# A fused recurrence and two gated MLPs on one core: zero products in TensorE's early gaps, a one-byte waste output, a new order table

## The chip, the cores and the metric

One core of a Trainium2 chip. The metric is the device time of one launch in microseconds (us). Three runs of the kernel before took 920.43 to 921.10 us, median 921.01.

## What is computed

A gated linear recurrence per head (4 batches, 8 heads, 768 steps, head size 48), then two MLPs over 3072 tokens of width 384 with 2048 hidden units:

```
for t in range(S):
    state = alpha[:, :, t, :, None] * state + einsum('bhd,bhe->bhde', k[:, :, t], v[:, :, t])
    y[:, :, t] = einsum('bhd,bhde->bhe', q[:, :, t], state)
x = y as (3072, 384)
h = x @ w_in;  x = (h * tanh(softplus(h))) @ w_out      # first MLP
h = x @ w_in2; x = (h * cos(h)) @ w_out2                # second MLP
```

The weights come as 64-bit floats, the rest in fp32.

## The kernel before, in words

**Recurrence.** 12 chunks of 64 steps, each in two halves of the batch; (u, hb) is chunk u, half hb. For each of the 24 pieces the load queue (SP) brings alpha (`ld_a`), keys (`ld_k`), queries (`ld_q`) and values (`ld_v`, `ld_vt`). VectorE (DVE) forms the running products of alpha (`scan`, L405), their backward form (`scan2`, L423), scales keys (`keys`, L427) and queries (`queries`, L437). TensorE (PE) forms `scores` (L469), DVE masks them (`causal`, L477 to L480), PE makes `out_mm` (L490 to L494), transposes the keys (`turn`, L455) and makes the new state (`state_mm`, L552, L559), which `state_mul` (L579 to L583) scales. `guard` (L413, ScalarE or ACT) looks whether every alpha is large enough for this path: the sum of relu(0.79 - alpha) goes to `alow`, the elementwise result to a waste tile `junk` that nobody reads.

**MLPs.** Blocks of 512 tokens; each 128-wide slice of the hidden layer is one step. `mm1` (L631 to L633) makes h from x and the weights in nine one-pass products (x and the weights are each split in a high and a low fp32r part). ACT and DVE make the gate (`angle`, `sines`, `gated`), `act_c` (L670, L672) and `pool_c` (L677) split the result in two, and `mm2` (L692 to L694) adds nine products into three accumulators `acc0` to `acc2`. The first six slices of the first block are taken in pairs over 256 tokens: mm1(0) to mm1(2) need the recurrence's (0,0) and (0,1), mm1(3) to mm1(5) need (1,0) and (1,1).

**Bridge.** For chunks 0 to 3, `last_heads` (L499) and `fill` (L505) bring the last two heads to their place, `y_hi` (L513) and `y_lo` (L519) write the two parts of x, for which mm1 waits.

**Weights.** `ld_w` loads slice fc of a layer (768 KB), and six passes `conv_x`, `conv_s` (L322), `conv_b`, `conv_c` (L335), `conv_d` (L340 on DVE) and `conv_e` (L348) turn the 64-bit numbers into the high and low parts. Tables (`TOPS`, `SCALES`, `ROUNDS`, `LOWS`) choose the engine of each.

**What sets the order.** All pieces are listed with an engine, and the table `ORDER` (2398 numbers) gives the sequence in which they are written out; every engine and the load queue run their own pieces strictly in that sequence. `VCOPY`, `QPOOL`, `KPOOL`, `MULS`, `GLS`, `CASTS` choose engines for other pieces. `IDLE` is 0, so no `idle` piece (L617) is written out. Buffers tie the loads to the engines: there is one buffer for keys and one for alpha, so `ld_k` of a piece waits for `scores` and `turn` of the piece before, and `ld_a` for its `keys`.

Of the kernel before, what the change touches and what calls it, by code (L numbers as in the profile page):

```python
# [13 lines left out]
F32 = mybir.dt.float32  # L14
F32R = mybir.dt.float32r
# [96 lines left out]
)  # L112
VCOPY = {*range(0, 4), *range(6, 24)}
LOAD_K = 143.22
LOAD_Q = -93.756
LOAD_V = -90.03
# [123 lines left out]
def chunked_path(ctx: ExitStack, tc: tile.TileContext, q, k, alpha, v1, ve, vo, w1, w2, const, out):  # L240
# [5 lines left out]
    def stile(shape, dtype, tag, name):  # L246
        return sb.tile(shape, dtype, tag=tag, bufs=BUFS[tag], name=name)
# [906 lines left out]
```

## Time and profile before

| | |
|---|---|
| runs, median (range) | 921.01 us (920.43 to 921.10) |
| the profiled execution | 920.94 us, of which span 919.0 us from first to last instruction |
| TensorE (PE) busy | 892.6 us, 97% of the span |
| DVE, ACT, POOL busy | 584.7, 655.8, 310.6 us |
| mean granted clock of TensorE | 0.987 of full speed |

A granted clock of 1.00 is 2.4 GHz, 0.50 is 1.2 GHz. The page's row of 40 slices of 23 us shows the clock under 1.00 in the first two slices alone (0.8 and 0.6), and PE's first slice at 4 tenths busy, its second at 8; from the third on it is at 9, but for the last (7). So what is not yet filled lies in the first 50 us.

### The profile page before, as it was taken

The page shows a single profiled execution, that of the slowest core. Times are in us where ns is not written, and L with a number is a line of the kernel's source. Part 1 is how long each engine was busy: PE and PEld are TensorE (multiplying, and loading weights), DVE is VectorE, ACT ScalarE, POOL GpSimd, SP SyncE. Part 2 cuts the span into 40 slices and gives each one's busy share as a digit, 9 for nine tenths or more (in the row PEclk, how much of TensorE's full clock was granted, in tenths as well). Part 3 has the DMA queues.
Part 4 walks back from the last instruction along what each step waited for, and adds up shares of the span by engine and source line. Part 5 has one row for each costly group of instructions (what it writes and reads, how often), then busy time and mean ns, then how long its engine had stood idle before and what let it go on. Part 6 is the DMA issues. An engine that isn't in the chain of part 4 may idle for free.

```text
span 919.0 us, 15379 instructions
## 1 busy us (share of the span) xinstructions
PE 892.6 (97%) x6038; PEld 734.2 (80%) x6038; DVE 584.7 (64%) x863; ACT 655.8 (71%) x1032; POOL 310.6 (34%) x237
## 2 busy tenths in 40 slices
PE   4899999999999999999999999999999999999997
PEld 3788787878878888788888888888888888888886
DVE  7999987575556467543687986865545445444552
ACT  3799798887869978988999856566545646555552
POOL 3655454121225033433266563333212124011021
PEclk8699999999999999999999999999999999999999
DMA  8866411212112213220133221200000000000001
GB/s 238 261 191 210 136 30 44 72 56 63 59 51 83 69 55 97 74 78 1 39 102 100 70 70 35 69 0 36 12 24 0 35 1 1 35 0 1 35 1 36
DMA packets 25325, 59.08 MB, mean 64 GB/s; under 512 B 3872, under 2 KB 7840, under 8 KB 25248
## 3 DMA queue, kind: packets, MB, share of 16 engines
q1 hardware_dynamic: 25104, 57.92, 20.2%
q8 instruction: 48, 0.79, 0.4%
q14 instruction: 29, 0.24, 0.1%
q10 hardware_dynamic: 144, 0.13, 0.0%
HBM read 52.53 MB, written 4.72 MB: 62 GB/s over the span
## 4 chain that ended last, share of the span: by engine, by line
PE 91%; DVE 4%; DMA 2%; ACT 1%; issue 1%; SPq 1%; DVEq 0%; ACTq 0%
PE h L631 14%; PE acc L692 14%; PE acc L694 14%; PE acc L693 14%; PE h L633 14%; PE h L632 14%; PE y L493 2%; PE sc L469 2%; DMA qt<-in_q_chunks_dram 1%; PE dS L559 1%; PE pt L455 1%; DVE wr L322 1%; DMA vt<-in_v_chunks_dram 1%; DVE wr L335 1%; DVE Pt L405 0%
## 5 line engine op out<-in xcount | busy, mean ns | idle before, releaser
L677 POOL TENSOR_TENSOR gl<-ta,gh 128x512 fp32r<-128x512 f32 x97 | 142.0, 1466 | 374.0 <-DVE gh L670 201.7
L631 PE MATMUL h<-xhi,wh 128*128 128x512 f32 (+1 forms) x594 | 233.2, 393 | 0.0
L692 PE MATMUL acc<-gh,wh 128*128 128x512 f32 (+1 forms) x594 | 229.9, 387 | 0.0
L633 PE MATMUL h<-xhi,wl 128*128 128x512 f32 (+1 forms) x594 | 229.0, 385 | 0.0
L632 PE MATMUL h<-xlo,wh 128*128 128x512 f32 (+1 forms) x594 | 228.9, 385 | 0.0
L694 PE MATMUL acc<-gl,wh 128*128 128x512 f32 (+1 forms) x594 | 227.5, 383 | 0.0
L693 PE MATMUL acc<-gh,wl 128*128 128x512 f32 (+1 forms) x594 | 227.4, 383 | 0.0
L631 PEld LDWEIGHTS h<-xhi,wh 128*128 128x128 f32 x594 | 113.0, 190 | 23.6 <-DVE ta L647 0.7
L633 PEld LDWEIGHTS h<-xhi,wl 128*128 128x128 f32 x594 | 113.0, 190 | 22.3
L632 PEld LDWEIGHTS h<-xlo,wh 128*128 128x128 f32 x594 | 113.1, 190 | 20.6
L692 PEld LDWEIGHTS acc<-gh,wh 128*128 128x128 f32 x594 | 111.6, 188 | 22.4 <-issue 0.6
L694 PEld LDWEIGHTS acc<-gl,wh 128*128 128x128 f32 x594 | 111.6, 188 | 22.2
L693 PEld LDWEIGHTS acc<-gh,wl 128*128 128x128 f32 x594 | 111.6, 188 | 21.2
L659 DVE SCALAR_TENSOR_TENSOR tb<-tb,ta 128x512 f32<-128x512 f32 x96 | 79.9, 833 | 74.4 <-ACT tb L656 74.3
L652 ACT ACTIVATE ta<-h 128x512 f32<-128x512 f32 x96 | 57.3, 597 | 84.5 <-PE h L633 48.4
L647 DVE TENSOR_TENSOR ta<-h,ta 128x512 f32<-128x512 f32 x96 | 64.9, 685 | 58.8 <-ACT ta L644 58.3
L677 DVE TENSOR_TENSOR gl<-ta,gh 128x512 fp32r<-128x512 f32 x95 | 75.4, 794 | 34.0 <-ACT gh L672 31.1
L662 ACT ACTIVATE tb<-tb 128x512 f32<-128x512 f32 x96 | 60.4, 629 | 48.3 <-DVE tb L659 48.3
L665 DVE TENSOR_TENSOR ta<-h,tb 128x512 f32<-128x512 f32 x96 | 66.0, 687 | 30.3 <-ACT tb L662 29.9
L670 DVE CAST gh<-ta 128x512 fp32r<-128x512 f32 x106 | 54.7, 519 | 43.4 <-PE acc L693 42.6
L672 ACT CAST gh<-ta 128x512 fp32r<-128x512 f32 x86 | 52.7, 616 | 32.3 <-PE acc L693 27.9
L639 ACT ACTIVATE ta<-h 128x512 f32<-128x512 f32 x96 | 57.4, 597 | 25.2 <-PE h L633 15.5
(152 smaller groups left out, 1202.1 us busy)
## 6 DMA issues: line engine op xcount, KB each, us to landing
wr<-in_w_dram SPq DMA_DIRECT2D x16, 768.0 KB, 5.8
three<-in_w_dram SPq DMA_DIRECT2D x16, 768.0 KB, 4.2
at<-in_alpha_chunks_dram SPq DMA_DIRECT2D x23, 227.9 KB, 2.8
qt<-in_q_chunks_dram SPq DMA_DIRECT2D x23, 224.0 KB, 3.4
kt<-in_k_chunks_dram SPq DMA_DIRECT2D x23, 224.0 KB, 2.7
vt<-in_v_chunks_dram SPq DMA_DIRECT2D x21, 192.0 KB, 2.8
out_dram<-o SPq DMA_DIRECT2D x14, 256.0 KB, 2.0
three<-in_ve_chunks_dram SPq DMA_DIRECT2D x24, 128.0 KB, 3.5
```

The lines of the kernel that those rows point to most:

```text
L631: nc.tensor.matmul(h, hi[:, f], xh, start=kc == 0, stop=False)
L632: nc.tensor.matmul(h, hi[:, f], xl, start=False, stop=False)
L633: nc.tensor.matmul(h, lo[:, f], xh, start=False, stop=kc == 2)
L639: nc.scalar.activation(ta_[i], h_[i], AF.Sigmoid, scale=-1.0)
L647: nc.vector.tensor_tensor(ta_[i], h_.pop(i), ta_[i], op=ALU.mult)
L659: nc.vector.scalar_tensor_tensor(out=tb_[i], in0=tb_[i], scalar=MAGIC, in1=ta_[i], op0=ALU.subtract, op1=ALU.subtract)
L662: nc.scalar.activation(tb_[i], tb_[i], AF.Sin, scale=-TWO_PI)
L665: nc.vector.tensor_tensor(ta_[i], h_.pop(i), tb_.pop(i), op=ALU.mult)
L677: eng.tensor_tensor(gl_[i], ta_.pop(i), gh_[i].bitcast(F32)[:, :], op=ALU.subtract)
L692: nc.tensor.matmul(acc[d][:, c0:c1], hi[:, f], gh, start=first, stop=False, skip_group_check=True)
L693: nc.tensor.matmul(acc[d][:, c0:c1], lo[:, f], gh, start=False, stop=False, skip_group_check=True)
L694: nc.tensor.matmul(acc[d][:, c0:c1], hi[:, f], gl, start=False, stop=last, skip_group_check=True)
```

## The change

- `idle` gets operands of its own: a tile of 128x128 zeros, written once by POOL, is both the weights and (four times repeated) the 512 moving columns of a one-pass product into the bank of `acc0`. `IDLE` goes from 0 to 60; an `idle` that comes in the order behind the first mm2 writes nothing, so 22 products are written out.
- `guard` multiplies by a million before the relu, and its waste output is one byte wide instead of two.
- `ORDER` and all tables that choose engines are new. The last 724 numbers of the order are those of before. Two estimates inside the planner change (`turn`, `fill`), which do nothing when the order is read from the table.

```diff
-    (the 2398 numbers of ORDER)
+    (2420 numbers, 22 of them idle pieces)
...
-VCOPY = {*range(0, 4), *range(6, 24)}
+VCOPY = {*range(0, 24)}
...
-LOWS = {*((0, fc) for fc in (2, 4, 7, 10, 13, 14,)), *((1, fc) for fc in (1, 4, 5, 7, 8, 11, 12, 13,))}
+LOWS = {*((0, fc) for fc in (0, 3, 5, 7, 9, 10, 11, 13, 14, 15,)), *((1, fc) for fc in (0, 1, 2, 4, 6, 7, 8, 11, 12, 13,))}
...
-IDLE = 0
+IDLE = 60
...
-TOPS = "aaaappaaappavvpp", "aapapppvavaapava"
-SCALES = "vvaaaaaaapavppvv", "vpvvvpapvppppvpa"
-ROUNDS = "vppaaavvpapapppa", "vvvpvpvpaapavpvv"
+TOPS = "avpvvaaaapavpppv", "vvpvpvapvvpvpava"
+SCALES = "vaaapapapvvaavaa", "vvaavpvpvppvpvpa"
+ROUNDS = "aavaaappaavppvvp", "pppvapvppaaavpvv"
...
+    zeros = sb.tile([P, P], F32R, name="zeros")
+    nc.gpsimd.memset(zeros.bitcast(F32), 0.0)
...
-    nc.vector.memset(abias, AOK)
+    nc.vector.memset(abias, 1e6 * AOK)
...
-        junk = stile([112, NSEG, C], BF16, "junk", "junk")
+        junk = stile([112, NSEG, C], mybir.dt.uint8, "junk", "junk")
...
-        nc.scalar.activation(junk, seg3(at_[s])[:, :, 1:65], AF.Relu, scale=-1.0, bias=abias[:112], accum_out=alow[:, n : n + 1])
+        nc.scalar.activation(junk, seg3(at_[s])[:, :, 1:65], AF.Relu, scale=-1e6, bias=abias[:112], accum_out=alow[:, n : n + 1])
...
-            nc.tensor.matmul(w[0:112], seg_start[:, 0:112], seg_start[:, 0:N], start=True, stop=True, skip_group_check=True)
+            nc.tensor.matmul(w.rearrange("p (a b) -> p a b", b=P), zeros, zeros.unsqueeze(1).to_broadcast([P, 4, P]), start=True, stop=True, skip_group_check=True)
```

**First place: the load queue's first rows.** Names as in the program: `at` is alpha, `big` holds all of piece (0,1), `wr` the raw weights. Before, then changed:

```order
L367 DMA at<-in_alpha_chunks_dram 112x521
L367 DMA big<-in_alpha_chunks_dram 112x521
L377 DMA qt<-in_q_chunks_dram 112x512
L959 DMA cst<-in_const_dram 128x272
L372 DMA kt<-in_k_chunks_dram 112x512
L380 DMA three_73<-in_ve_chunks_dram 64x512
L381 DMA three_73<-in_vo_chunks_dram 64x512
L372 DMA big<-in_k_chunks_dram 112x512
L303 DMA wr<-in_w_dram 128x1536
L367 DMA at<-in_alpha_chunks_dram 112x521
L377 DMA big<-in_q_chunks_dram 112x512
L303 DMA wr<-in_w_dram 128x1536
```
```order
L370 DMA at<-in_alpha_chunks_dram 112x521
L370 DMA big<-in_alpha_chunks_dram 112x521
L306 DMA wr<-in_w_dram 128x1536
L380 DMA qt<-in_q_chunks_dram 112x512
L375 DMA kt<-in_k_chunks_dram 112x512
L375 DMA big<-in_k_chunks_dram 112x512
L962 DMA cst<-in_const_dram 128x272
L383 DMA three_75<-in_ve_chunks_dram 64x512
L384 DMA three_75<-in_vo_chunks_dram 64x512
L380 DMA big<-in_q_chunks_dram 112x512
L394 DMA vt<-in_v_chunks_dram 128x384
L370 DMA at<-in_alpha_chunks_dram 112x521
```

The first weights moved from ninth to third place, ahead of the first queries and keys; the values `vt` that the first state products read moved ahead of the second alpha and the second weights.

**Second place: PE, from the first out_mm to the first state products** (`y` is out_mm's bank, `dS` the state's, `zeros` the fill operand). Before, then changed:

```order
L491 MATMUL y<-three_74,three_73 64x64
L455 MATMUL pt<-cst,big 128x112 x4
L559 MATMUL dS_192<-vt,kT 48x48 x2
L559 MATMUL dS_193<-vt,kT 48x48 x2
L505 MATMUL y<-st_180,cst 32x128 x6
```
```order
L494 MATMUL y<-three_76,three_75 64x64
L623 MATMUL acc_200<-zeros 128x512
L623 MATMUL acc_203<-zeros 128x512
L623 MATMUL acc_206<-zeros 128x512
L623 MATMUL acc_209<-zeros 128x512
L623 MATMUL acc_212<-zeros 128x512
L623 MATMUL acc_216<-zeros 128x512
L562 MATMUL dS_219<-vt,kT 48x48 x2
```

Six fill products now stand between the two; five more stand ahead of everything, four ahead of fill(0,0), two ahead of out_mm(0,1), four ahead of mm1(0), and one ahead of state_mm(0,1).

**Third place: DVE's last rows up to keys(2,0), and PE's around the first mm2.** (`ta<-h,ta` is gated(0), `gl` is pool_c(0), `wl` a conv_e, the last `kt` keys(2,0).) DVE before, then changed:

```order
L579 TENSOR_TENSOR three_73<-dS_460,aend 48x4x48 x2
L579 TENSOR_TENSOR three_73<-dS_461,aend 48x4x48 x2
L405 SCALAR_TENSOR_TENSOR Pt<-at,seg_start 112x520
L322 SCALAR_TENSOR_TENSOR wr<-wr 128x768
L647 TENSOR_TENSOR ta<-h,ta 128x512
L409 RECIPROCAL rend<-Pt 112x8
L335 SCALAR_TENSOR_TENSOR wr<-wr 128x768
L423 SCALAR_TENSOR_TENSOR at<-at,rend 112x520
L427 TENSOR_TENSOR kt<-kt,at 112x512
L348 TENSOR_TENSOR wl<-wr,wh 128x768
L677 TENSOR_TENSOR gl<-ta,gh 128x512
```
```order
L351 TENSOR_TENSOR wl<-wr,wh 128x768
L650 TENSOR_TENSOR ta<-h,ta 128x512
L338 SCALAR_TENSOR_TENSOR wr<-wr 128x768
L412 RECIPROCAL rend<-Pt 112x8
L680 TENSOR_TENSOR gl<-ta,gh 128x512
L338 SCALAR_TENSOR_TENSOR wr<-wr 128x768
L426 SCALAR_TENSOR_TENSOR at<-at,rend 112x520
L430 TENSOR_TENSOR kt<-kt,at 112x512
L351 TENSOR_TENSOR wl<-wr,wh 128x768
```

PE before (the end of scores(2,0), fill(1,1), mm2(0)), then changed (the end of mm1(1), fill(1,1), scores(2,0)):

```order
L470 MATMUL sc<-three_73,kt 64x64
L505 MATMUL y<-st_585,cst 32x128 x6
L692 MATMUL acc_603<-gh,wh 128x256
L693 MATMUL acc_603<-gh,wl 128x256
L694 MATMUL acc_603<-gl,wh 128x256
```
```order
L634 MATMUL h<-xhi,wh 128x256
L635 MATMUL h<-xlo,wh 128x256
L636 MATMUL h<-xhi,wl 128x256
L508 MATMUL y<-st_599,cst 32x128 x6
L472 MATMUL sc<-three_75,kt 64x64
```

pool_c(0) moved ahead of keys(2,0) on DVE, and on PE fill(1,1) ahead of scores(2,0), so that mm2(0) follows scores(2,0) at once.

## Rows read from the trace of the kernel before

**Rows 1.** Windows: engines' busy us (instructions), granted clock, DMA share, GB/s
```profile
17.90:35.20 17.30, 15.09 (x202) 13.16 (x203) 15.59 (x21) 10.91 (x21) 9.81 (x7) 0.51 0.94 271
35.20:50.00 14.80, 11.02 (x184) 9.51 (x184) 14.55 (x21) 12.15 (x22) 7.87 (x5) 0.77 0.72 229
50.00:70.00 20.00, 19.30 (x294) 17.20 (x290) 18.98 (x31) 18.87 (x29) 11.97 (x7) 1.00 0.59 183
70.00:100.00 30.00, 29.58 (x404) 25.15 (x403) 27.84 (x39) 24.32 (x42) 16.03 (x13) 1.00 0.59 193
100.00:110.00 10.00, 9.55 (x80) 7.11 (x77) 9.78 (x12) 9.38 (x14) 5.91 (x5) 1.00 0.27 81
```
**Rows 2.** Waits of PE, 110 to 900 us: who for whom, total, times, longest
```profile
PE y L493 <- ACT st L530: 1.1, 1, 1.1
```
**Rows 3.** DVE in order of time: start, us, line, operation [idle before <- releaser]
```profile
19.00 0.95 DVE L335 SCALAR_TENSOR_TENSOR wr<-wr 128x768 uint32<-128x768 uint32 x1
...
21.98 0.56 DVE L340 CAST wh<-wr 128x768 fp32r<-128x768 f32 x1
...
23.79 2.15 DVE L335 SCALAR_TENSOR_TENSOR wr<-wr 128x768 uint32<-128x768 uint32 x1
...
34.59 1.37 DVE L427 TENSOR_TENSOR kt<-kt,at 112x512 f32<-112x512 f32 x1 [0.93 <-DMA kt<-in_k_chunks_dram]
...
48.95 0.69 DVE L427 TENSOR_TENSOR kt<-kt,at 112x512 f32<-112x512 f32 x1
...
50.43 0.69 DVE L677 TENSOR_TENSOR gl<-ta,gh 128x512 fp32r<-128x512 f32 x1
```
**Rows 4.** PE in order of time, 14 to 52 us
```profile
18.46 0.89 PE L559 MATMUL dS<-vt,kT 64*48 64x48 f32 x32 [3.54 <-DMA vt<-in_v_chunks_dram]
...
32.34 0.58 PE L631 MATMUL h<-xhi,wh 128*128 128x256 f32 x1
...
33.15 0.41 PE L631 MATMUL h<-xhi,wh 128*128 128x256 f32 x1
33.36 0.41 PE L632 MATMUL h<-xlo,wh 128*128 128x256 f32 x1
...
35.04 0.28 PE L631 MATMUL h<-xhi,wh 128*128 128x256 f32 x1
...
49.79 0.24 PE L469 MATMUL sc<-three,kt 48*64 48x64 f32 x1 [0.50 <-DVE kt L427]
...
50.87 0.84 PE L505 MATMUL y<-st,cst 48*32 48x128 f32 x12
51.65 0.39 PE L692 MATMUL acc<-gh,wh 128*128 128x256 f32 x1
```
**Rows 5.** Loads issued from 26 to 29 us: KB, us from issue to landing
```profile
kt<-in_k_chunks_dram SPq DMA_DIRECT2D x1, 224.0 KB, 8.4
```
**Rows 6.** Windows of 5 us, columns as in rows 1
```profile
15.00:20.00 5.00, 1.54 (x40) 1.38 (x42) 4.84 (x7) 1.00 (x5) 3.66 (x2) 0.79 1.07 255
20.00:25.00 5.00, 4.44 (x63) 3.67 (x60) 4.32 (x6) 3.84 (x10) 2.37 (x1) 0.50 0.74 209
25.00:30.00 5.00, 3.91 (x60) 3.40 (x60) 4.96 (x6) 3.30 (x5) 4.01 (x4) 0.50 0.99 284
```
**Rows 7.** PE in order of time, steady stage, into an out_mm
```profile
172.36 0.39 PE L632 MATMUL h<-xlo,wh 128*128 128x512 f32 x1
172.59 0.39 PE L633 MATMUL h<-xhi,wl 128*128 128x512 f32 x1
172.91 0.27 PE L493 MATMUL y<-three 128*64 128x64 f32 x1
```
**Rows 8.** Window, columns as in rows 1: attention products alone
```profile
22.00:24.00 2.00, 2.00 (x34) 1.73 (x34) 2.00 (x5) 1.00 (x3) 1.37 (x1) 0.50 0.82 184
```
**Rows 9.** POOL and ACT in order of time: a conv_e, and a guard
```profile
22.63 2.50 POOL L348 TENSOR_TENSOR wl<-wr,wh 128x768 fp32r<-128x768 f32 x1 [3.96 <-DVE wh L340]
...
3.75 0.72 ACT L415 ACTIVATE junk<-at,abias 112x512 bf16<-112x512 f32 x1 [1.73 <-DMA at<-in_alpha_chunks_dram]
```

More of the change, by code (lines that the diff above doesn't have):

```diff
@@ L126 @@
 FILL = 4
-QPOOL = {1, *range(4, 6), *range(7, 9), 12, 15, *range(19, 23)}
-MULS = {3, 5, *range(7, 9), *range(10, 13), 14, 18, *range(20, 22)}
-LOWS = {*((0, fc) for fc in (2, 4, 7, 10, 13, 14,)), *((1, fc) for fc in (1, 4, 5, 7, 8, 11, 12, 13,))}
-GLS = {0, *range(2, 9), *range(12, 14), *range(17, 22), *range(23, 25), 26, *range(28, 31), 33, *range(35, 37), 39, 41, *range(45, 47), *range(48, 50), 51, 53, *range(55, 58), 63, *range(68, 70), 72, 74, *range(76, 78), *range(83, 85), 88, *range(91, 94), *range(98, 100), 101, 106, *range(111, 113), *range(114, 116), 117, *range(121, 124), *range(126, 128), 130, *range(134, 139), 140, *range(142, 144), 146, *range(150, 152), 153, 157, *range(159, 163), *range(164, 166), 169, *range(173, 178), *range(179, 181), *range(185, 188), 189, *range(191, 193), *range(194, 199)}
-IDLE = 0
-KPOOL = {1, 6, *range(8, 11), *range(13, 16), 17, 19, 23}
-TOPS = "aaaappaaappavvpp", "aapapppvavaapava"
-SCALES = "vvaaaaaaapavppvv", "vpvvvpapvppppvpa"
-ROUNDS = "vppaaavvpapapppa", "vvvpvpvpaapavpvv"
+QPOOL = {*range(3, 6), *range(7, 13), 14, 18, 21, 23}
+MULS = {3, 5, *range(7, 9), 10, 12, *range(14, 16), *range(19, 22)}
+LOWS = {*((0, fc) for fc in (0, 3, 5, 7, 9, 10, 11, 13, 14, 15,)), *((1, fc) for fc in (0, 1, 2, 4, 6, 7, 8, 11, 12, 13,))}
+GLS = {0, *range(2, 4), 7, *range(10, 14), 15, 18, 20, *range(22, 24), *range(26, 28), *range(29, 31), 33, 35, *range(37, 40), 41, 43, 46, 48, 52, *range(54, 61), 62, *range(64, 66), *range(67, 69), *range(70, 72), 73, *range(75, 78), *range(79, 83), 84, *range(92, 94), *range(96, 99), *range(100, 105), 106, *range(111, 113), *range(114, 116), 117, *range(121, 124), *range(126, 128), 130, *range(134, 139), 140, *range(142, 144), 146, *range(150, 152), 153, 157, *range(159, 163), *range(164, 166), 169, *range(173, 178), *range(179, 181), *range(185, 188), 189, *range(191, 193), *range(194, 199)}
+IDLE = 60
+KPOOL = {1, 6, 9, *range(11, 14), 15, 18, 22}
+TOPS = "avpvvaaaapavpppv", "vvpvpvapvvpvpava"
+SCALES = "vaaapapapvvaavaa", "vvaavpvpvppvpvpa"
+ROUNDS = "aavaaappaavppvvp", "pppvapvppaaavpvv"
 TICK, BUSY = 10.24 / 3, 3060
@@ L138 @@
 QUARTER = float(np.nextafter(np.float32(np.pi / 2), np.float32(0.0)))
-CASTS = {*range(0, 3), *range(4, 8), 11, 13, *range(16, 18), 19, 26, *range(28, 30), *range(34, 36), *range(37, 39), *range(42, 45), *range(46, 50), *range(51, 53), 54, 56, 58, *range(63, 65), *range(67, 70), 72, *range(79, 82), 86, 89, 95, *range(98, 101), *range(102, 104), 106, 109, 116, *range(118, 121), *range(122, 124), *range(125, 127), *range(129, 131), *range(134, 138), 141, *range(143, 145), 147, *range(151, 154), *range(156, 160), 163, 165, 167, *range(169, 171), *range(173, 175), 178, 181, 185, 189, 192, *range(194, 200)}
+CASTS = {0, 2, *range(5, 8), 9, *range(11, 13), *range(19, 21), 22, *range(24, 27), 28, 30, 36, 38, 41, 48, 52, *range(55, 57), 58, *range(64, 68), 69, 74, 78, 81, 85, 87, 90, 95, 97, 99, *range(102, 104), *range(105, 107), 109, 116, *range(118, 121), *range(122, 124), *range(125, 127), *range(129, 131), *range(134, 138), 141, *range(143, 145), 147, *range(151, 154), *range(156, 160), 163, 165, 167, *range(169, 171), *range(173, 175), 178, 181, 185, 189, 192, *range(194, 200)}
 PAIR = 2
@@ L927, in chunked_path @@
         if not end:
-            add(("turn", s), PE, pe(0.31, 0.4, 0.1), d + 3.2 + LATE * (u == 0), f(turn, s), [("const",), ("keys", s), ("queries", s)] if e else [("const",), ("keys", s)], [(pdrop, ("pt", n))] + ([] if e else [("kT", ("kT", n))]), ex if e else [("kt", n)])
+            add(("turn", s), PE, pe(0.33, 0.4, 0.1), d + 3.2 + LATE * (u == 0), f(turn, s), [("const",), ("keys", s), ("queries", s)] if e else [("const",), ("keys", s)], [(pdrop, ("pt", n))] + ([] if e else [("kT", ("kT", n))]), ex if e else [("kt", n)])
             add(("turned", s), ACT, 0.48, d + 4 + LATE * (u == 0), f(turned, s), [("turn", s)], [], [("pt", n)])
@@ L934, in chunked_path @@
             add(("last_heads", s), ACT, 0.2, d - FILLED + 8, f(last_heads, s), [("out_mm", s)], [("st6", ("st6", s))])
-            add(("fill", s), PE, pe(0.7, 0.15, 0.25), d - FILLED + 8.3, f(fill, s), [("last_heads", s)], [], [("st6", s)])
+            add(("fill", s), PE, pe(0.75, 0.15, 0.4), d - FILLED + 8.3, f(fill, s), [("last_heads", s)], [], [("st6", s)])
         if u < FILL:
@@ L956, in chunked_path @@
     for j in range(IDLE):
-        cost = pe(0.3)
+        cost = pe(0.2267)
         add(("idle", j), PE, lambda now, cost=cost: (0.0, 0.0) if begun else cost(now), 1e6 + j, idle, [("idle", j - 1)] if j else [("ones",)])
```

121 rows, old and new, of the table ORDER are left out of this document.

## The prediction

> **What bounds the kernel now.** I read the windows first. From 50 us on PE is the bound: it idles 0.70, 0.42 and 0.45 us in the three windows up to 110 us [rows 1], and from 110 to 900 us it waits once, 1.1 us, for an ACT copy that frees a bank [rows 2]. After 50 us a change can therefore gain only these 2.7 us, or by taking work off PE. Ahead of 50 us PE is not the bound. From 17.9 to 50 us it is idle 2.21 + 3.78 = 6.0 us, and the granted clock is 0.51 and 0.77 [rows 1]. Since it is either 1.00 (2.4 GHz) or 0.50 (1.2 GHz), that is 17.30 x 0.49 x 2 = 17.0 us and 14.80 x 0.23 x 2 = 6.8 us at the low level. In the same windows DVE is busy 15.59 of 17.30 and 14.55 of 14.80 us, and the loads take 0.94 and 0.72 of the DMA engines [rows 1]. So the start is set by loads and DVE, and what a faster PE is worth there has to be asked link by link.
>
> The last link I take from the time lines. scores(2,0) at 49.79 had idled 0.50 us for keys(2,0), which DVE ran at 48.95; behind it stand fill(1,1) at 50.87 and mm2(0) at 51.65 [rows 3, 4]. From there PE runs practically without a break, so **whatever moves mm2(0) moves the end**. Going back along DVE, its queue is without a wait from keys(1,1) to keys(2,0); keys(1,1) at 34.59 had waited 0.93 us for its load [rows 3], which had been 8.4 us under way [rows 5]. The chain ahead of mm2(0) is loads up to 34.6 us, then DVE.
>
> **The change part by part.**
>
> *The load of keys(1,1).* Counting the load queue's rows in both orders, the same 23 transfers go out up to and including this one; only their sequence differs. It can land earlier only where the queue runs dry. It does once: 209 GB/s in 20 to 25 us, between 255 and 284 [rows 6]. A steady 270 would have taken 5 x 209/270 = 3.9 us, so 1.1 us are lost there. The queue then stands for keys(1,0), whose end frees the alpha buffer. In the new order the two 128 KB value loads of (0,1) stand behind the key load of (1,0), no longer ahead of it: 262 kB at 255 GB/s, 1.0 us earlier. That fills most of the hole; I take **-0.8 us**, ends 0 and -1.1.
>
> *keys(1,1) itself* took 1.37 us against 0.69 for keys(2,0) [rows 3], beside a POOL pass. POOL's passes are different now, but not gone: half of it, **-0.3 us**, ends 0 and -0.7.
>
> *DVE from keys(1,1) to keys(2,0)*, counted off the order: one conv_s less (I price it as conv_c, 0.95), a conv_d cast (0.56) and pool_c(0) (0.69) more [rows 3]: **+0.3 us**. keys(2,0) and scores(2,0) so come 0.8 us earlier.
>
> *fill(1,1) ahead of scores(2,0).* It now runs while PE waits for keys(2,0), so mm2(0) follows scores(2,0) directly: 51.65 - 50.87 = **-0.8 us** [rows 4]. If scores(2,0) were no longer waited for, this would be worth nothing.
>
> *Later waits.* Of the 2.7 us I take a third away, **-0.9 us**: DVE enters that stage with pool_c(0) behind it, and two state copies move to ACT (`VCOPY`), but DVE is still busy 18.98 of 20 us up to 70 us [rows 1], so something will be late again. The order up to its last 724 numbers is new, and unread waits can come as well as go: ends -2.7 and +2.7.
>
> *Changes between the recurrence and the MLPs on PE.* From product to product it takes 172.59 - 172.36 = 0.23 us, into an out_mm 0.32 [rows 7], 0.09 us more. Counting the two orders, PE changes kind 115 times, before 123: 8 x 0.09 = **-0.7 us**, ends 0 and -1.
>
> *The fill products.* None is in the trace of before. At 2.4 GHz the nearest row is a 128x512 product: a start every 0.23 us, 0.39 us from start to end [rows 7]. All 22 write one bank, each waiting for the one before, so 0.39 is the price. At 1.2 GHz 256 columns start every 33.36 - 33.15 = 0.21 us and take 0.41 [rows 4], so 512 take about 0.62. The five first ones run while PE has nothing. The other 17 cost 6.6 to 10.5 us of PE ahead of mm2(0). I count them at nothing, because what stands behind them has another reason to be late: the six ahead of state_mm(0,0) lie in the 3.54 us for which it waited for its values [rows 4], and if they hold the clock up, the 15.09 us that PE worked from 17.9 to 35.2 us [rows 1] shrink by nearly half and cover them all. If they don't, see the third rival.
>
> *Does the clock follow?* In 22 to 24 us PE was busy all 2.00 us with attention products alone, and the clock stayed at 0.50 [rows 8]; in mm1(0), begun at 32.34, a product's time fell from 0.41 to 0.28 us by 35.04 [rows 4]. So full-array products raised it, and small ones did not, though PE was as busy. The Trainium skill, TensorE: Matmul & The Clock Gate, Part 1, says that the throttled state is the default and that the engine's activity releases it, busy-ness being what is watched. By that alone the attention products should have held the clock; the rows say otherwise, and I go by the rows, under which whole-array zeros are the right filler. By the rule the fills would be superfluous and the sum the same.
>
> *conv_e from POOL to DVE.* In the first layer six move to DVE and two to POOL. A conv_c beside the POOL conv_e that ran from 22.63 for 2.50 us [rows 9] took 2.15 us, alone 0.95 [rows 3]: 1.2 us of DVE lost, against some 0.95 for a conv_e on DVE itself. Net four: 4 x (0.95 - 1.2) = -1.0 us of DVE, most of it behind mm2(0), where PE is the bound; I take 0. The Trainium skill, SBUF — State Buffer, calls the port pair of the two an exclusive lock, the later one blocking fully; the conv_c, 1.2 us late and ending 0.8 us behind the conv_e, agrees.
>
> *The rest.* guard's ACTIVATE took 0.72 us for 2-byte output [rows 9]; with one byte that row stays the nearest; even a third more or less in each of the 24 lies on an ACT that isn't late: 0. The zeros' memset precedes POOL's first use by far: 0. The first weights ahead of the first queries and keys (768 KB) delay scores(0,0) by some 1 to 2 us, which the wait for values above covers.
>
> **Sum.** -0.8 - 0.3 + 0.3 - 0.8 - 0.9 - 0.7 = -3.2 us against the profiled execution's 920.94: 917.7. The median of the runs is 0.07 above that execution, so I forecast **917.8 us** (own range 915.8 to 919.8).
>
> **Rivals.**
>
> *More comes.* All 2.7 us of waits go (1.8 more), and DVE is freed of one whole collision as the one above (1.2): 914.8. For it: fewer POOL conv_e. Against: DVE's share up to 110 us.
>
> *Nothing comes.* Loads and DVE give mm2(0) at the same time as before, a new wait eats the changes' saving, and only fill(1,1)'s 0.8 us is left: 920.2. For it: 0.94 of the DMA engines up to 35 us, and terms that are all under 1 us.
>
> *Slower: the fill products run at 1.2 GHz and make PE late.* Place: the twelve ahead of scores(1,0), whose end (with turn) frees the key buffer for the load of keys(1,1). At the low clock they take 12 x 0.62 = 7.4 us. PE was busy 4.44 and 3.91 of 5 us in 20 to 30 us at that clock [rows 6], so there are under 2 us for them there, and about 3 in the gap ahead of state_mm(0,0): some 2.5 us are left over, and the key load, keys(1,1) and mm2(0) come that much later, 921.0 + 2.5 = 923.5. It decides at one point: if scores(1,0) ends after about 28 us. At full clock the same row of work costs some 6 us less, and there is no delay. Against it: nothing in rows shows zeros as the operand, but that the clock rose under dense whole-array products speaks for the fills.
>
> That the change does nothing at all is not a case: the order moves the first loads.
>
> **How the numbers follow.** A measurement here can tell about 0.2% (1.8 us) from no change, so faster is under 919.2 and slower above 922.9. Forecast 0.50 (0.43 of it faster, 0.07 same), more 0.13 (faster), nothing 0.21 (0.03 faster, 0.17 same, 0.01 slower), slower 0.16 (0.02 same, 0.14 slower). Together: faster 0.59, same 0.26, slower 0.15. The range goes from 914.5, just under the better case, to 922.5, which leaves out most of the slower case and the far ends of the later waits.
>
> **What would show it.** Right: granted clock near 1.00 from 18 to 35 us; keys(1,1) starting at 33.5 to 34; scores(2,0) at about 49.0 and mm2(0) at about 50 instead of 51.65; less than 2 us of idle PE from 55 to 900 us; steady products still 0.23 us apart. Wrong: a clock of 0.50 from 20 us on with the fill products 0.6 us each and scores(1,0) past 28 us (slower); mm2(0) at 51 to 52 (nothing); or new waits of PE of 1 us and more between 55 and 500 us, which the order alone does not let me see.

## The result, and the profile after

The changed kernel took 930.77 us (median of 4 runs, 929.77 to 933.72); the kernel before, beside it on the same chip, 920.72 us. The ratio is 1.0115, 95% interval 1.009 to 1.0141: **1.15% slower**, outside the range and on the side of the third rival, though for the most part not by its mechanism. The profiled execution, the shortest of the four, has a span of 928.0 us against 919.0.

Two things differ: the start is later, and from 110 us on the products simply stand further apart. First the windows of the changed kernel (busy us of PE, PEld, DVE, ACT, POOL with instruction counts, granted clock, DMA share, GB/s), to set beside [rows 1]:

```profile
17.90:35.20 17.30, 16.58 (x215) 11.02 (x216) 15.06 (x21) 8.65 (x19) 7.81 (x4) 1.00 0.83 262
35.20:50.00 14.80, 12.52 (x222) 10.88 (x223) 13.98 (x21) 11.67 (x21) 5.00 (x5) 0.88 0.84 266
50.00:70.00 20.00, 18.05 (x233) 16.36 (x230) 16.05 (x25) 14.91 (x24) 7.41 (x8) 0.83 0.50 167
...
600.00:700.00 100.00, 100.00 (x439) 82.05 (x438) 55.45 (x84) 59.55 (x102) 27.29 (x19) 1.00 0.04 16
700.00:800.00 100.00, 100.00 (x438) 82.06 (x437) 50.16 (x75) 55.97 (x95) 24.84 (x18) 1.00 0.02 9
```

The same windows of the kernel before, late in the run:

```profile
600.00:700.00 100.00, 100.00 (x443) 82.81 (x442) 52.64 (x81) 58.19 (x99) 25.78 (x18) 1.00 0.04 16
700.00:800.00 100.00, 100.00 (x443) 82.77 (x442) 50.74 (x76) 57.45 (x98) 24.78 (x18) 1.00 0.05 17
```

The reader should see that PE is busy all 100 us in both, at full clock, and yet gets 438 or 439 products through where it did 443. From start to start (mean over 600 to 900 us) a 128x512 product takes 0.2289 us instead of 0.2267. That is too little to be seen in two neighbouring rows, where both kernels show 0.23, but there are 3,348 such products. (From 110 to 400 us the two means lie closer, 0.2293 against 0.2279, so the loss is smaller than 3,348 times 0.0022 us.) "PE busy" doesn't tell it either: only the count does.

PE of the changed kernel in order of time, beside [rows 4] (a product of zeros is `acc<-zeros`):

```profile
0.99 4.21 PE L623 MATMUL acc<-zeros 128*128 128x512 f32 x5 [0.99 <-POOL zeros L262]
...
18.19 0.31 PE L493 MATMUL y<-three,three 64*64 64x64 f32 x1
...
19.82 3.86 PE L623 MATMUL acc<-zeros 128*128 128x512 f32 x6
...
25.44 2.15 PE L623 MATMUL acc<-zeros 128*128 128x512 f32 x4
...
29.80 0.22 PE L493 MATMUL y<-aux,three 64*64 64x64 f32 x1
...
31.50 0.22 PE L472 MATMUL sc<-three,kt 48*64 48x64 f32 x1
...
52.48 0.34 PE L472 MATMUL sc<-three,kt 48*64 48x64 f32 x1 [1.95 <-DVE kt L430]
...
54.38 0.58 PE L695 MATMUL acc<-gh,wh 128*128 128x256 f32 x1
...
75.37 0.36 PE L695 MATMUL acc<-gh,wh 128*128 128x256 f32 x1
```

The two `y` rows are products of out_mm: 0.31 us at 18.19, as at the low level, 0.22 us at 29.80. The 1.00 in the first of the windows above therefore holds only from about 21.5 us on, where the products of zeros fall from 0.80 to 0.50 us.

DVE of the changed kernel, keys(1,1) and keys(2,0), beside [rows 3]:

```profile
36.31 0.68 DVE L430 TENSOR_TENSOR kt<-kt,at 112x512 f32<-112x512 f32 x1
...
51.64 0.69 DVE L430 TENSOR_TENSOR kt<-kt,at 112x512 f32<-112x512 f32 x1
```

scores(1,0) ends at 31.7 instead of 26.0, keys(1,1) starts 1.7 us later than before, keys(2,0) 2.7 us, mm2(0) 2.7 us (54.38 against 51.65), and mm2(1) 3.8 us (75.37 against 71.60). Behind that the loss is not in waits, as PE's own list of them shows:

```profile
PE y L496 <- ACT st L533: 0.2, 1, 0.2
```

This is the changed kernel's only wait of PE between 110 and 900 us, 0.2 us; before it was 1.1 us [rows 2]. So the order did what was forecast there, and the time was lost in the pace.

### The profile page after: what moved, and what is told of

It reads as the page before. It is cut to its first block, busy times and chain, and to the rows that moved or that the text cites. A ratio compares the mean times of both kernels' runs of the same rounds, so it can differ in the third digit from the quotient of the medians.

```text
span 928.0 us, 15408 instructions
## 1 busy us (share of the span) xinstructions
PE 905.6 (98%) x6060; PEld 735.7 (79%) x6060; DVE 600.6 (65%) x883; ACT 647.2 (70%) x1026; POOL 277.2 (30%) x220
## 4 chain that ended last, share of the span: by engine, by line
PE 89%; ACT 4%; DMA 1%; issue 1%; POOL 0%; DVE 0%; POOLq 0%; ACTq 0%
PE h L634 14%; PE acc L695 14%; PE acc L697 14%; PE h L636 14%; PE acc L696 14%; PE h L635 14%; PE y L496 2%; PE sc L472 2%; PE dS L562 1%; PE pt L458 1%; ACT L642 1%; ACT ta L647 1%; DMA at<-in_alpha_chunks_dram 1%; ACT ta L642 0%; ACT L647 0%
## 5 line engine op out<-in xcount | busy, mean ns | idle before, releaser
L680 POOL TENSOR_TENSOR gl<-ta,gh 128x512 fp32r<-128x512 f32 x88 | 124.4, 1414 | 400.0 <-DVE gh L673 180.1
L697 PE MATMUL acc<-gl,wh 128*128 128x512 f32 (+1 forms) x594 | 230.5, 388 | 0.0
L680 DVE TENSOR_TENSOR gl<-ta,gh 128x512 fp32r<-128x512 f32 x104 | 80.6, 777 | 29.6 <-ACT gh L675 25.5
```

The lines of the kernel that those rows point to most:

```text
L680: eng.tensor_tensor(gl_[i], ta_.pop(i), gh_[i].bitcast(F32)[:, :], op=ALU.subtract)
L697: nc.tensor.matmul(acc[d][:, c0:c1], hi[:, f], gl, start=False, stop=last, skip_group_check=True)
```

## The experiments

The first expectations name theories by letter. For the pace: A, the addresses at which the tiles lie; its rivals look for it in the new order or in the rest of the edit, and want it unchanged when only addresses change. For the start: S1, the products of zeros make PE late; S2, the order of the loads and of DVE does. The address of a tile is that of the compiled program. The changed order first uses the tiles in another sequence, the waste tile is half as large and `zeros` is new, so wh lies at 68640 (before 77408), wl at 117792 (126560), xlo at 177248 (179040), while xhi, gh and gl stay.

**Addresses alone, in both directions.** A helper takes each tile once, at the program's start, in a given sequence, which fixes the address (shortened):

```diff
+    hold("qt", ...); hold("kt", ...); hold("Pt", ...); hold("junk", ...)
+    zeros = sb.tile([P, P], F32R, name="zeros")
+    hold("wh", ...); hold("wl", ...); hold("kT", ...); hold("vt", ...); hold("xlo", ...)
```

e1 is the changed kernel so laid out as before (`zeros` in the freed half of `junk`):

> The changed kernel with every SBUF tile at the address that it had before (order, fill products and one-byte waste output as changed; the zeros lie in the half of the waste tile that is free now). Two losses are to be explained: mm2(0) came 2.7 us later and mm2(1) 3.8 us later than before, and from 110 us to the end three products take 0.687 us where they took 0.680. Theory A (addresses): the pace goes with where weights, x and gate tiles lie; expected 0.680 us for three products, mm2(0) still at about 54 us, time about 923.5 us. Theory B (the fill products, or the one-byte output, or the order itself slow the products down): pace stays 0.687, time about 930. Theory C (it is the chip of that run): pace 0.687 here and in the kernel before beside it.

Measured: 926.99 us, ratio 1.0055 [1.0038, 1.0071], pace 0.2267. One part missed: mm2(0) came at 58.49 us, not at about 54. In this execution PE stayed at the low level until 35.8 us, where the attention products fall from 0.31 to 0.22 us, and 17 of the 22 products of zeros took about 0.80 us:

```profile
L642 PE MATMUL acc<-zeros x22: 494/796/796, 3.2 to 44.9; 128*128 128x512 f32 x22
```

```profile
18.71 5.06 PE L642 MATMUL acc<-zeros 128*128 128x512 f32 x6
...
26.94 3.33 PE L642 MATMUL acc<-zeros 128*128 128x512 f32 x4
...
32.31 1.63 PE L642 MATMUL acc<-zeros 128*128 128x512 f32 x2
...
35.64 0.31 PE L492 MATMUL sc<-three,kt 48*64 48x64 f32 x1
...
35.85 0.22 PE L492 MATMUL sc<-three,kt 48*64 48x64 f32 x1
```

scores(1,0) so ended at 36.8 us, against 31.7 in the changed kernel's execution, which has the same order and the same zeros. e2 is the reverse, the kernel before with the changed one's addresses:

> The kernel before, old order, no fill products, with the tiles at the changed kernel's addresses and the guard's one-byte output. Theory A (addresses): start as before (mm2(0) at 51.7 us), three products 0.687 us from 110 us on, time about 921 + 7.5 = 928.5 us. Theory B (fill products or new order): pace 0.680, time 921. If the one-byte output were the cause, the pace would be slow only while guards run, up to about 300 us.

Measured: 927.7 us, ratio 1.0072 [1.0052, 1.0091], pace 0.2289; mm2(0) at 52.50. The first row is e1's window, the second e2's:

```profile
600.00:700.00 100.00, 100.00 (x443) 82.84 (x442) 56.26 (x85) 59.89 (x102) 27.48 (x19) 1.00 0.04 16
```

```profile
600.00:700.00 100.00, 100.00 (x439) 82.05 (x438) 52.66 (x81) 57.52 (x98) 25.88 (x18) 1.00 0.04 16
```

The pace follows the addresses whichever order and instructions stand on them. A holds; its rivals fall.

**Without the products of zeros.** e3 is the changed kernel, e4 the same with the addresses of before:

```diff
-        if not acc_:
+        if False:
```

> The changed kernel without its 22 products of zeros, which no result reads; order and addresses as changed. Theory S1 (the fill products, 0.56 to 0.64 us each, are what makes the start late: 12 of them, 7 us, lie ahead of scores(1,0)): scores(1,0) ends 3 us or more earlier than 31.7 us, mm2(0) at about 52, time 2 to 3 us less than the changed kernel's. Theory S2 (the new sequence of loads and of DVE's passes makes it late): scores(1,0) at most 1 us earlier, mm2(0) at 54 or later, time the same or, with the clock at 0.50 again, some us more. Pace: theory A 0.687; theory B (fill products) 0.680.

> Both: addresses of before, no products of zeros, order as changed. With theory A and S1: pace 0.680, mm2(0) at about 52, time about 920 to 921. With A and S2: pace 0.680, mm2(0) at 54 or later, time 923 to 925. With B: as the run without fill products.

Measured: e3 930.24 us, 1.0087 [1.007, 1.0104]; e4 923.99 us, 1.0024 [1.0012, 1.0035]. Against e4, e1 says that the zeros cost 0.3%. Against e3, the changed kernel says the same (0.28%), but those two intervals overlap. In the changed kernel's own execution S1 is not what makes scores(1,0) late: without the zeros it still ends at 32 us in e3 and 30.7 in e4. In e1's they do make it late: e4 differs from e1 by the zeros alone, and in its execution scores(1,0) ended 6 us earlier. Each is one profiled execution, and in the two with zeros, of the same order, the clock rose at different times; why is not shown. Something in the new order and its engine tables remains, 0.24%.

**Which address.** e5 to e8 are the kernel before with the one-byte guard, in which only wh and wl are shifted, by a pad below and one above:

```diff
+    sb.tile([P, 448], mybir.dt.uint8, name="below")
     hold("wh", ...); hold("wl", ...)
+    sb.tile([P, 64], mybir.dt.uint8, name="above")
```

> The kernel before with its order and without fill products; the guard has one byte, and every tile lies where it lay before, except the weight tiles wh and wl, which lie 64 bytes lower, so that their addresses leave 32 on division by 512 as in the changed kernel (before: 96). Theory W (the weights' address sets the pace of the products): 600 to 900 us at 0.2289 us a product instead of 0.2267, some 6.5 us more in all, 927 to 928. Rival X (the pace comes from another tile's address, xlo or the attention tiles, or from the one-byte guard): 0.2267, 920.5 to 921.5.

> As e5_weights_32, but the weights' addresses leave 0 on division by 512. Theory W says only that the pace changes with this number; whether 0 is better than 96 is open: a pace below 0.2267, each 0.001 us of it worth 3.6 us, if full alignment is what counts, 0.2289 or more if the distance to the moving tiles counts. Rival X: 0.2267, 920.5 to 921.5.

> As e5_weights_32, but the weights' addresses leave 64 on division by 512. Theory W: if alignment to 64 bytes is what counts, the same pace as with 0; if 128 bytes count, another than with 0. Rival X: 0.2267, 920.5 to 921.5.

> As e5_weights_32, but the weights' addresses leave 224 on division by 512, which is 96 on division by 128, as before. Theory W with a period of 128 bytes: 0.2267 as before, 920.5 to 921.5; with a period of 256 or 512 bytes: another pace, up to 0.2289 and 928. Rival X: 0.2267 as well, so it is told apart by the three others only.

All four left 0.2267, so it is the weights' address (rival X falls), and three were far worse than the changed kernel: e6 940.98, e7 941.46 and e8 939.41 us, while e5 took 927.86. A period of 128 bytes falls with e8. Then the two other distances, and the weights together with the moving tiles:

> As e5_weights_32, but the weights' addresses leave 352 on division by 512, as those of the moving tiles (xhi, xlo, gh, gl) do. If the pace hangs on the difference of the two addresses with a period of 256 bytes, 352 is the same as 96: 0.2267 us a product and 920.5 to 922.5. If the period is 512 bytes, another pace, between 0.2133 (512 columns at 2.4 GHz and nothing else) and 0.2333.

> As e5_weights_32, but the weights' addresses leave 160: 64 bytes on the other side of 96. If only the distance from the moving tiles counts, whichever way, 0.2289 as with 32 and 927 to 928; if the direction counts, another pace, up to 0.2333 and 941.

> The kernel before with the one-byte guard, weights and moving tiles (with all that lies above them) all 96 bytes lower than before: the weights leave 0, the moving tiles 256, and their distance is as before. Theory D (the distance between the two sets the pace): 0.2267 and 920.5 to 922.5, although the weights leave 0 as in e6_weights_0 (0.2333). Theory S (the weights' own address sets it): 0.2333 and 941.

e9 took 920.78 us (0.9984 [0.9965, 1.0003]), e10 942.97, e11 921.35 (0.999 [0.9969, 1.0011]). e6 and e11 have the same weight addresses; only the moving tiles differ. The first row is e6's, the second e11's:

```profile
600.00:700.00 100.00, 100.00 (x431) 80.43 (x430) 54.51 (x82) 56.68 (x97) 29.97 (x20) 1.00 0.04 17
```

```profile
600.00:700.00 100.00, 100.00 (x443) 82.81 (x442) 52.58 (x81) 58.20 (x99) 25.74 (x18) 1.00 0.04 16
```

(With them e11 shifts all that lies above them, which the products from 600 to 700 us do not read.) Theory D holds: what counts is the distance between the two operands. The last two values:

> As e5_weights_32, but the weights' addresses leave 128 on division by 512, so that the moving tiles lie 224 bytes behind them modulo 256. Six of the eight distances that the 32-byte steps of the addresses allow are measured: 0 gives 0.2267 us, 64 gives 0.2289, 32, 96, 128 and 192 give 0.2333. If only 0 and 64 escape, 0.2333 and 941; a shorter pace than 0.2267 would make a kernel faster than both, 3.6 us for each 0.001.

> As e14_weights_128, with the weights' addresses leaving 192 (distance 160, the last of the eight). If only 0 and 64 escape, 0.2333 and 941.

e14 took 941.6 us, e15 944.58. The whole table, pace as the mean from start to start between 600 and 900 us:

| moving tile's address minus weights', modulo 256 | us a product | kernel | ratio to before |
|---|---|---|---|
| 0 | 0.2267 | before, e9, e11 | 1, 0.9984, 0.999 |
| 32 | 0.2333 | e7 | 1.0205 |
| 64 | 0.2289 | changed (1.0115), e2, e5 | 1.0072, 1.0058 |
| 96 | 0.2333 | e6 | 1.0199 |
| 128 | 0.2333 | e8 | 1.0182 |
| 160 | 0.2343 | e15 | 1.0243 |
| 192 | 0.2333 | e10 | 1.0224 |
| 224 | 0.2333 | e14 | 1.0211 |

The kernel before already stood on the best of the eight, so none of these beats it by what can be measured. e9 and e11 also show that the one-byte guard costs nothing.

**What is left of the start.** e12, e13 and e16 build on e4. e12 puts the first weights' load back, and their conversion with it:

```diff
 ld_a(0,0) ld_a(0,1)
-ld_w(0,0)
 ld_q(0,0) ld_k(0,0) ld_k(0,1)
+ld_w(0,0)
```

> The changed kernel with the addresses of before and without the 22 products of zeros (e4_layout_before_no_fill), and with the first weight tile's load put back behind the first keys' loads, its four steps of conversion behind keys(0,1). If the first weights ahead of the first queries and keys are what makes the start late: scores(0,0) back from 12.9 to 9.5 to 10.5 us, mm2(0) from 53.3 to 50.5 to 52 and the whole 921 to 922.5, ratio 1.000 instead of 1.0024. If the prediction was right that the wait for values covers this: mm2(0) within 0.5 us of 53.3 and 924.

Measured: 923.55 us, 1.0013 [0.9999, 1.0027], which overlaps e4. scores(0,0) does come at 9.03, but then queries(0,1) wait 3.75 us for their load, and mm2(0) stands at 53.23 against 53.32. This agrees with the prediction: the delay of the first scores was covered.

e13 moves one piece on PE (as e16 below, with scores(1,0) alone):

> The changed kernel with the addresses of before and without the products of zeros (e4_layout_before_no_fill), with one piece moved on PE: scores(1,0), which the change put behind fill(0,0), turn(0,1) and out_mm(0,1), goes back ahead of these three. In e4 scores(1,0) ended at 30.7 us (before: 25.95), and fill(0,1) behind it at 31.8, for whose cast DVE stood idle 1.22 us. If this place is what makes the start late: scores(1,0) ends at 24 to 25.5 us, the load of keys(1,1) is issued 5 to 6 us earlier, fill(0,1) ends at 30 to 30.6, keys(1,1) starts at 34.0 to 34.7 instead of 35.6, mm2(0) at 51.5 to 52.5 instead of 53.3, and the whole 922 to 923 (ratio 1.000 to 1.001). If DVE's own work is what makes it late: keys(1,1) and mm2(0) within 0.4 us of e4 and 924 (1.0024).

Measured: 926.56 us, 1.0045 [1.0028, 1.0062]. That is slower than e4: the intervals overlap a little, but its shortest run, 925.76 us, is longer than e4's longest, 925.32. The rows say why; they are of the longest of its four runs, 929.83 us. The first is scores(1,0). The releaser that it names, a reciprocal that had just begun, is not the real one. The second row, the weight load of the same product, names it: ACT's `turned`, the third row. Two banks hold the attention's sums in that stage, and scores(1,0) had to wait until the one with turn(1,0) was emptied.

```profile
28.96 0.37 PE L491 MATMUL sc<-three,kt 48*64 48x64 f32 x1 [6.03 <-DVE rend L431]
28.96 0.18 PEld L491 LDWEIGHTS sc<-three,kt 48*64 48x64 f32 x1 [6.25 <-ACT kT L482]
...
28.38 0.53 ACT L482 COPY kT<-pt 128x448 f32<-128x448 f32 x1
```

So e13 told nothing of the place itself. e16 takes that wait away by the order of ACT:

```diff
 PE:  scores(0,1) 
+PE:  turn(1,0) scores(1,0)
+ACT: turned(1,0), directly behind queries_odd(1,0)
 PE:  fill(0,0) turn(0,1) out_mm(0,1)
-PE:  scores(1,0)
```

> As e13_scores_earlier, but turn(1,0) and turned(1,0) go up as well: on PE scores(0,1), turn(1,0), scores(1,0), fill(0,0); on ACT turned(1,0) directly behind queries_odd(1,0). In e13 scores(1,0) stood until 28.96 us, when turned(1,0) ended on ACT (28.38 + 0.53) and gave its bank free; now that copy ends some 5 us earlier. If the place of scores(1,0) is what makes the start late: it ends by 25.5 us, the load of keys(1,1) is issued 5 us earlier than in e4, and mm2(0) comes at 51.5 to 52.5, the whole at 922 to 923 (1.000 to 1.001). If the work and the waits on DVE set keys(2,0) whatever PE does: out_mm(0,1) now waits for y_lo(0,0) on DVE to free the other bank (about 28.1), fill(0,1) ends no more than 0.6 us earlier than in e4 (31.8), mm2(0) at 52.7 or later, the whole at 923.4 to 924.5 (1.0018 to 1.003).

Measured: 924.22 us, 1.0022 [1.001, 1.0033], the same as e4. Here scores(1,0) ended at 25.9 us as before the change, and the load of keys(1,1) went out at 26.52 instead of 30.78. Yet keys(1,1) did not come earlier. These rows are the keys(1,1) of e4 and its window up to there; then the same of e16; then the window of the kernel before up to its keys(1,1) (columns as above, the third count is DVE's):

```profile
35.60 0.68 DVE L449 TENSOR_TENSOR kt<-kt,at 112x512 f32<-112x512 f32 x1
...
0.00:35.60 35.60, 17.28 (x260) 15.18 (x262) 28.38 (x40) 14.75 (x31) 12.93 (x16) 0.90 0.85 246
```

```profile
36.52 0.67 DVE L449 TENSOR_TENSOR kt<-kt,at 112x512 f32<-112x512 f32 x1
...
0.00:36.52 36.52, 18.31 (x241) 15.52 (x242) 28.27 (x41) 14.79 (x30) 11.66 (x16) 0.84 0.89 247
```

```profile
0.00:34.59 34.59, 19.96 (x270) 17.31 (x271) 26.94 (x37) 15.69 (x33) 16.24 (x19) 0.76 0.91 254
```

keys(1,1) no longer waits for its load in e4, e16 and the changed kernel. (In e16 that load, issued 4.3 us earlier than in e4, was 8.2 us under way instead of 2.9, and so landed no earlier: at 34.7 against 33.7 us.) DVE works 28.1 to 28.4 us ahead of keys(1,1), where it worked 26.9. Of the weights' conversion it has three conv_x (1.6 us), a conv_e (0.95 us) and a conv_s more, which ACT and POOL had before or which came later; it has queries(0,1) for 1.67 us in place of queries(1,1) for 0.67; and other passes that are shorter or gone give back two thirds of it. (POOL has 12.93 or 11.66 us there instead of 16.24.) I take this extra work for the late step, but that is argued: what DVE would give without it was not tried.

## Why the prediction was wrong

In the profiled executions the 9.0 us are made up of 3.8 up to mm2(1) and 5.2 behind it (928.0 - 75.37 = 852.6 against 919.0 - 71.60 = 847.4). e2 loses 5.5 there by addresses alone (924.8 - 71.92 = 852.9). In ratios, from the changed kernel by e1 and e4 to before: addresses 0.60%, zeros 0.31%, order 0.24%.

- **"The rest. ... with one byte that row stays the nearest ... 0."** This is the step that failed most. The guard itself was costed rightly; that a smaller waste tile, a new tile and a new first use move the weights' tiles against the tiles that stream past them was not seen. It cost 5.5 us of 10, more than any term in the sum. The forecast sign "steady products still 0.23 us apart" was too coarse to show it. That the kernel before stood on the best distance was luck of its layout.
- **Fill products, counted at nothing.** The clock was forecast near 1.00 from 18 us on; it came from about 21.5 us on in the changed kernel's profiled execution, and from 35.8 us on in e1's. The prices were too low. The forecast was 0.39 us each at 2.4 GHz and about 0.62 at 1.2 GHz; the runs show about 0.50 and 0.80. The changed kernel's tile view (minimum, median, maximum in ns), and the weight load of the second product of zeros:

```profile
L623 PE MATMUL acc<-zeros x22: 480/500/797, 1.0 to 39.8; 128*128 128x512 f32 x22
```

```profile
1.85 0.29 PEld L623 LDWEIGHTS acc<-zeros 128*128 128x128 f32 x1 [0.56 <-PE acc L623]
```

  All write one bank, each as a new tile, so each waits for the one before, as forecast; but its weight load waits too (the last row), and that was left out of the price. The twelve ahead of scores(1,0) took 7.0 us in the changed kernel, which is nearly the third rival's 7.4 for the low clock, and 10.0 us in e1. That what stands behind them is late anyway was true of the one (e3 without zeros is as late) and not of the other. In the medians they cost 0.3%, by e1 and e4.
- **Does the clock follow?** I concluded from [rows 8] that small attention products don't raise the clock. The 0.79 from 15 to 20 us in [rows 6] already spoke against it, since mm1 began only at 32.34 us (turn(0,1), begun at 14.18 in that trace, took 0.74 us, turn(0,0) at 11.34 took 1.01). e12 has no zeros, and there it rose in the middle of scores(0,1), behind nothing but work of the attention:

```profile
17.86 0.31 PE L492 MATMUL sc<-aux,big 48*64 48x64 f32 x1
...
18.07 0.23 PE L492 MATMUL sc<-aux,big 48*64 48x64 f32 x1
...
18.26 0.22 PE L492 MATMUL sc<-aux,big 48*64 48x64 f32 x1
```

  e4, without one zero, rose in the middle of scores(0,1) too (0.31 us up to 20.86, 0.26 at 20.96), and read 1.00 from 35.2 to 50 us. The Trainium skill, TensorE: Matmul & The Clock Gate, Part 1, which I set aside, says that activity of the engine releases the clock; these rows agree with it.
- **"The load of keys(1,1)", -0.8, and keys(1,1) itself, -0.3.** The load landed at 34.58 us instead of 34.50, so the first term came to nothing, and its premise was wrong: once the order changed, keys(1,1) did not wait for that load. I counted DVE's pieces only behind keys(1,1); ahead of it there were 1.2 to 1.4 us more. What is late next was not asked. keys(1,1) itself took 0.68 us instead of 1.37, all of the -0.7 that was the far end of its range.
- **DVE from keys(1,1) to keys(2,0), +0.3.** Without keys(1,1) itself the work grew by 1.0 us (from 14.11 - 1.37 to 14.42 - 0.68). One conv_s, begun while POOL ran a pass, took 1.64 us where I had priced 0.95. From start to start the stretch took 15.33 us instead of 14.36; about 0.7 us of that are new waits.
- **fill(1,1) ahead of scores(2,0), -0.8.** It came in e16, where mm2(0) follows keys(2,0) after 54.66 - 52.74 = 1.9 us instead of 2.7. In the changed kernel it was eaten: PE had idled 1.95 us for keys(2,0), the clock read 0.72 from 50 to 55 us, and scores(2,0) and mm2(0) ran at the low level.
- **Later waits, -0.9, and changes of kind, -0.7.** Behind mm2(1) the new order is 0.3 to 0.4 us faster (e4: 921.1 - 74.05 = 847.05 against 847.4). The waits went nearly as forecast, from 1.9 to 0.9 us in the changed kernel and 1.3 in e4, between 75.5 and 900 us. Of the 0.7 for fewer changes of kind nothing is seen.
- **First weights, covered.** Right, by e12.
- **The third rival** named the point rightly, scores(1,0) past 28 us, and a time of 923.5; the point was passed. It laid this on zeros at the low clock. That is what happened in e1's execution. In the changed kernel's own, scores(1,0) is as late without the zeros (e3), and an early scores(1,0) alone did not bring keys(1,1) forward (e16).

## What to carry to other kernels

When a change adds, removes or resizes a tile, or changes which tile is used first, compare the addresses of the tiles that the hot instructions read, and count instructions in a window of steady work: a loss of 1% can sit under a busy share of 100%. Test an edit with the addresses held fixed before its order is judged. And where a wait is to be removed, count the queue ahead of the waiting instruction as carefully as that behind it.

## What the runs showed of the hardware

- Products of 512 columns in one stream, each with a weight load that begins as the product ahead of it streams, took 0.2267 to 0.2343 us in the mean by the distance between the two operands' addresses modulo 256 bytes, nothing else changed. The order of the distances has no simple form: 0 is best, 64 next, the others much alike. Both operands moved together leave the pace as it was (e11), so the two reads act on one another; in what way was not shown. The Trainium skill, SBUF — State Buffer, SBUF: two separate sides, says that PE never waits on anyone; whether this loss is a wait in that sense is open, but by that sentence alone one would not look for 3% of PE's pace in an address. The Trainium skill, TensorE: Matmul & The Clock Gate, Part 1, gives 215.7 ns from start to start for 512 columns at 2.4 GHz; no run's mean here came under 226.7.
- The record of the granted clock reads 1.00 in the first 17.6 us of every run, yet attention products take 0.31 us there and 0.22 later at the same reading (e12's rows above). In e1 it reads 1.00 from 17.9 to 35.2 us as well, beside products of zeros of 0.80 us. Up to the first recorded change the durations tell the clock, not the record.
- A product's row can name the wrong releaser: in e13 it was a DVE instruction with which the bank had nothing to do, while the row of the weight load named the right one.
